# A recurrence with routed experts: when the chosen rows are numbered, fetched and turned

## The chip, the cores and the metric

The kernel runs on one core of a Trainium2 chip. The time is device microseconds of one execution; the profile is the hardware profiler's record of one execution. The core has five instruction queues that run beside each other, each in its own order: PE (matrix products and transposes), DVE (VectorE), ACT (ScalarE), POOL (GpSimd) and SP (SyncE, which here only issues DMAs). Queues wait for each other by semaphores.

## The reference, cut to what matters

Two blocks follow each other. The first is a linear-attention recurrence over 768 tokens, for 4 batches and 8 heads of width 48, with a state per head:

```
for t in range(S):
    cur   = einsum('bhd,bhe->bhde', u * k[t], v[t])
    y[t]  = einsum('bhd,bhde->bhe', r[t], state + cur)
    state = w * state + einsum('bhd,bhe->bhde', k[t], v[t])
```

The heads of y are laid side by side to x (4 batches, 768 tokens, 384 columns). The second block sends only some tokens of each batch through an MLP:

```
scores = einsum('bsd,d->bs', x, w_gate)
out = x.copy()
for b in range(B):
    top_idx = argpartition(-scores[b], capacity)[:capacity]      # capacity = 128
    xe = x[b, top_idx]
    ye = maximum(xe @ w1, 0) @ w2                                # w1: 384 x 1024
    out[b, top_idx] = xe + sigmoid(scores[b, top_idx])[:, None] * ye
```

## The kernel before, in words

**Blocks and steps.** Each batch has NC = 6 blocks of 128 tokens, so there are NU = 24 blocks. The main loop (L626) has 25 steps. Step i finishes the y of block i-1, computes scores and states of block i, turns k and r of block i+1, and works on the gate scores of blocks i-1 and i-2. Loads are issued by SP at the head of a step: k and r of block i+4 (`load_kr`, L85, L86), v of block i+3 (`load_v`, L97 or L101), in steps 4 to 12 also parts of w1 and w2 (`weights`, L208, L210), and the store of an earlier y (`store_y`, L345).

**One step, engine by engine.** PE: products from the state (L297 with z), score products k by r (`score_product`, L268), when experts are under way also state products (L278), products with the values (L297 with vin), otherwise the state products here (L292), the turn of k (L249, bank pt), the turn of r (L249, bank ea or st), pieces of the experts (`hidden`, L482; `expert`, L492), the turn of a score column (`score_row`, L379). ACT: half of the mask's diagonal (`diagonal`, L235), decays of the state (L328), copies of y (`leave_y`, L340, L341), the copy of turned k (L259). DVE: the masked copy of the scores (`masked`, L312), which writes into the mask tile `at` that ACT and POOL have filled; new states z and g (L317, L322); scaling of turned r (L254); the bonus sum `du` of the next block (L228), from which the next mask is made; the gate score (L354); comparisons of scores (L368, L385). POOL: the other half of the mask's diagonal (`diagonals`, L243, from block 4 on); then the products `kw`, `rk` and `rku` of block i+2 (L218, L222, L224).

**Choosing rows.** A token's rank in its batch is the number of scores that are at least its own. `against_earlier` and `against_own` write comparisons as 0 and 1, `count` (L395) sums them on PE, `rank` (L402, L403) adds parts of the sum on DVE, `one_hot` (L411) marks which token has which rank, `picked` (L418) turns the marks into token numbers by six small products, `index` (L424) adds their two parts to an integer, and `fetch` (L431, L432) reads the 128 rows back from `out` by an indirect DMA that POOL issues. `chosen` turns these rows on PE (L449) and copies them on ACT to `xt` (L451), and `enqueue` puts the pieces of the MLP into a queue, from which later steps take equal shares (`pieces`). `gate_sum` and `gate` (L464, L468) compute the sigmoid; `leave` (L505) and `send` (L523) add and write the rows back.

**What sets the order.** Every engine's order is the order in which the program issues instructions. Work of the second block is put into a step by hand: `at(step, place, function, ...)` files it, and `run(i, place)` issues what is filed for step i at that place. Batch b's last block is e = 6b + 5; its ranks are made in step e+3 (8, 14, 20), its rows fetched in step e+4 (9, 15, 21), its experts begun in step e+5 (10, 16, 22). The last batch is handled by code of its own behind the loop. The places of a step, in order, are "rows" (behind the masks and decays), "gate", then the masked copy and the states, "start", the turn of k, "between", the turn of r, "turned", "pick", the bonus sum, the gate score, "middle" and the rest. Whether experts are under way (`late`) is decided at the head of the step, from the queue.

PSUM banks are named; `free_bank` (L362) gives `picked`, `chosen` and `score_row` the bank ea while eb holds expert sums, and eb otherwise. A product into a bank waits until the bank's last reader is done.

Of the kernel before, what the change touches and what calls it, by code (L numbers as in the profile page):

```python
# [17 lines left out]
def kernel(  # L18
# [56 lines left out]
    def half(j):  # L75
        return slice(j * C, (j + 1) * C)

    def load_kr(n):
        b, c = divmod(n, NC)
        rows = slice(c * T, (c + 1) * T)  # L80
        if n == 0:
            KIN[n] = kws[NKW - 1][:, :, :D]
        else:
            KIN[n] = work.tile([128, H, D], F32, name="kin", bufs=NIN)
        nc.sync.dma_start(out=KIN[n], in_=k[b, :, rows, :].rearrange("h t d -> t h d"))  # L85
        nc.sync.dma_start(out=rpads[n % NIN][:, :, :D], in_=r[b, :, rows, :].rearrange("h t d -> t h d"))  # L86
# [6 lines left out]
    def load_v(n):  # L93
        b, c = divmod(n, NC)
        if n >= WHOLE:
            rows = slice(c * T, (c + 1) * T)
            nc.sync.dma_start(out=vins[n % NV][:, :, 0, :], in_=v[b, :, rows, :].rearrange("h t d -> t h d"))  # L97
            return
        for j in range(2):
            rows = slice(c * T + j * C, c * T + (j + 1) * C)  # L100
            nc.sync.dma_start(out=vins[n % NV][half(j), :, j, :], in_=v[b, :, rows, :].rearrange("h t d -> t h d"))  # L101
# [33 lines left out]
    for c in range(2):  # L135
        rows = slice(c * C, (c + 1) * C)
# [66 lines left out]
    def weights(n):  # L203
        for _ in range(n):
            j = parts.pop(0)
            if isinstance(j, tuple):
                f = slice(j[0] * F // 4, (j[0] + 1) * F // 4)
                nc.sync.dma_start(out=w1[:, j[1], f], in_=moe_w1[j[1] * 128 : (j[1] + 1) * 128, f])  # L208
            else:
                nc.sync.dma_start(out=w2[:, j, :], in_=moe_w2[j * 128 : (j + 1) * 128, :])  # L210
# [26 lines left out]
    def diagonals(n):  # L237
        if n not in AT:
            AT[n] = work.tile([128, H, C], F32, name="at", bufs=4)
        h = H // 2  # L240
        du = DU[n].rearrange("t i p -> t (i p)")
        eng = nc.gpsimd if n > 3 else nc.vector
        eng.tensor_mul(AT[n][:, h:, :], dia[:, None, :].to_broadcast([128, H - h, C]),  # L243
                       du[:, h:, None].to_broadcast([128, H - h, C]))
# [18 lines left out]
    def head(i):  # L263
        return slice(i * PAD, i * PAD + D)

    def score_product(n, hp, i, c):
        s = half(c)
        nc.tensor.matmul(out=RP[n][s, i, hp * C : (hp + 1) * C], lhsT=KH[n][head(i), hp, s],  # L268
                         rhs=RH[n][head(i), hp, s], start=True, stop=True, skip_group_check=True)
# [5 lines left out]
    def state_product(n, hp, i, c):  # L275
        if c and n % NC == NC - 1:
            return
        nc.tensor.matmul(out=RP[n][half(i), c, NP * C + hp * D : NP * C + (hp + 1) * D],  # L278
                         lhsT=kws[n % NKW][half(c), 2 * hp + i, :], rhs=vins[n % NV][half(c), 2 * hp + i, slot(n, c), :],
                         start=True, stop=True, skip_group_check=True)  # L280
# [20 lines left out]
    def from_state(n, hp, i, q):  # L301
        c = q ^ i
        z = Z1[n] if c else Z0.get(n)
        if z is not None:
            y_product(n, c, hp, i, RH[n][head(i), hp, half(c)], z[head(i), hp, :])
# [26 lines left out]
    def side(n, i):  # L332
        return YP[n][i][:, : NP * D].rearrange("t (p d) -> t p d", p=NP)
# [220 lines left out]
    def at(m, place, f, *a):  # L554
        fill.setdefault((m, place), []).append((f, a))

    def run(m, place):
        for f, a in fill.get((m, place), []):
            f(*a)
# [4 lines left out]
    for b in range(B - 1):  # L564
        e = b * NC + NC - 1
        if b:
            at(e + 3, "pick", count, b, range(NC), "st")
            at(e + 3, "middle", rank, b, ())
        else:
            at(e + 3, "turned", rank, b, range(NC), "eb")  # L570
        for z in range(NST):
            at(e + 3, "middle" if b else "turned", one_hot, b, z)
            at(e + 4, "rows", picked, b, z)
            at(e + 4, "start", index, b, z)
            at(e + 4, "start", fetch, b, z)
            at(e + 5, "between" if b else "rows", chosen, b, z)
            at(e + 5, "between" if b else "rows", enqueue, b, z)
            at(e + 5, "middle", gate_sum, b, z)
            at(e + 6, "gate", gate, b, z)

# [41 lines left out]
    def next_store(i, ahead):  # L622
        if i > 1 and ahead == ((i - 2) % NC >= NC - 2):
            store_y(i - 2)

    for i in range(NU + 1):  # L626
        next_store(i, True)
        if i + 4 < NU:
            load_kr(i + 4)
        if i + 3 < NU:  # L630
            load_v(i + 3)
        weights(WEIGHTS.get(i, 0))
        next_store(i, False)
        late = bool(queue)
        if not i:
            first()
            continue
        if i:
            if i < NU:
                t = psum.tile([128, 2, 512], F32, name="y")  # L640
                YP[i - 1] = [t[:, 0, :], t[:, 1, :]]
            else:
                YP[i - 1] = [psum.tile([128, 512], F32, name=name) for name in ("pt", "st")]
            for hp in range(NP):
                for j in range(2):
                    for q in (1, 0):
                        from_state(i - 1, hp, j, q)
            for j in range(1 if i < NU else 2):
                nc.scalar.copy(tiny[:, 1 : 1 + NP], side(i - 1, j)[C : C + 1, :, 0])
        if i < NU:  # L650
            if i not in RP:
                RP[i] = psum.tile([128, 2, 512], F32, name="rp")
            for hp in range(NP):
                for j in range(2):
                    for c in range(2):
                        score_product(i, hp, j, c)
            if late:
                for hp in range(NP):
                    for c in range(2):
                        for j in range(2):  # L660
                            state_product(i, hp, j, c)
        else:
            against_earlier(i - 2)
            score_row(i - 2, "y")
            against_own(i - 2)
            pieces(1)
        if i:
            for hp in range(NP):
                for c in range(2):
                    for j in range(2):  # L670
                        from_values(i - 1, hp, j, c)
        if i and i < NU:
            diagonal(i)
            if i > 3:
                diagonals(i)
            decays(i - 1)
            run(i, "rows")
            leave_y(i - 1)
            run(i, "gate")
        if i < NU:  # L680
            masked(i)
        if i < NU and not late:
            ST[i] = psum.tile([128, 512], F32, name="st")
            state_products(i)
        if i < NU:
            states(i)
        run(i, "start")
        if i + 1 < NU:
            if i:
                turned_k(i + 1, turn(kws[(i + 1) % NKW], "pt"))  # L690
            run(i, "between")
            turned(i + 1, turn(rpads[(i + 1) % NIN], "st" if late else "ea"))
        run(i, "turned")
        old = len(ready)
        leaving()
        m = share(i)
        if i < NU and m and (i, "pick") in fill:
            pieces(min(m, 2))
            m -= min(m, 2)
        run(i, "pick")  # L700
        if i + 1 < NU:
            bonus_sum(i + 1)
            if i < 3:
                diagonals(i + 1)
        if i and i < NU:
            gate_score(i - 1)
        run(i, "middle")
        if i < NU:
            pieces(m)
        if 2 <= i < NU:  # L710
            against_earlier(i - 2)
            score_row(i - 2, "st" if i == NC + 2 else None)
            against_own(i - 2)
        run(i, "last")
        if i + 1 < NU and not queue:
            unread(psum.tile([128, 512], F32, name="ea" if i == NC + 2 else "st"))
        run(i, "chosen")
        if i + 2 < NU:
            scaled(i + 2)
            bonus(i + 2)  # L720
        if i == 2:
            clear_v(5)
        if i == 4:
            numbers()
        send(old)
        run(i, "fetch")

    b, n = B - 1, NU - 1
# [66 lines left out]
```

## Time and profile before

| what | value |
|---|---|
| three runs | 165.79, 167.84, 171.86 us; median 167.84 us |
| the profiled execution | 168.37 us, its span 166.5 us |
| mean granted PE clock in it | 0.979 |
| busy: PE, DVE, ACT, POOL | 147.5, 117.4, 97.6, 103.5 us |
| moved by DMA | 24.13 MB, mean 145 GB/s |

How the lines are read: in a timeline or group, `L354 DVE SCALAR_TENSOR_TENSOR scr<-x,wg` is line 354 on DVE, writing tile `scr` from `x` and `wg`; ahead of it stand its start in the span and its length. `[0.91 <-POOL at L243]` says that the engine stood idle 0.91 us before it and that POOL's instruction of L243, writing `at`, ended this. PEld is the loading of weights for PE, POOLq and SPq are the queues that issue DMAs. A product in 32 bit counts as two PE instructions.

### The profile page before, as it was taken

The page shows a single profiled execution, that of the slowest core. Times are in us where ns is not written, and L with a number is a line of the kernel's source. Part 1 is how long each engine was busy: PE and PEld are TensorE (multiplying, and loading weights), DVE is VectorE, ACT ScalarE, POOL GpSimd, SP SyncE. Part 2 cuts the span into 40 slices and gives each one's busy share as a digit, 9 for nine tenths or more (in the row PEclk, how much of TensorE's full clock was granted, in tenths as well). Part 3 has the DMA queues.
Part 4 walks back from the last instruction along what each step waited for, and adds up shares of the span by engine and source line. Part 5 has one row for each costly group of instructions (what it writes and reads, how often), then busy time and mean ns, then how long its engine had stood idle before and what let it go on. Part 6 is the DMA issues. An engine that isn't in the chain of part 4 may idle for free.

```text
span 166.5 us, 8139 instructions
## 1 busy us (share of the span) xinstructions
PE 147.5 (89%) x3423; PEld 123.4 (74%) x3423; DVE 117.4 (70%) x315; ACT 97.6 (59%) x346; POOL 103.5 (62%) x138
## 2 busy tenths in 40 slices
PE   6899797999999539999979989999989799997990
PEld 3587585788788429998857869998767698746990
DVE  5659999889998924578676879866788797733010
ACT  6635787887886713476863893877648837301200
POOL 7989992999881890956682299988632831022022
PEclk9999999999999975999999999999999999999999
DMA  3999889959888778988597889999411212111000
GB/s 64 178 185 184 141 155 190 196 136 208 184 198 169 150 199 231 224 228 220 141 254 154 188 193 178 210 210 215 108 53 45 62 47 98 51 24 72 4 23 24
DMA packets 81990, 24.13 MB, mean 145 GB/s; under 512 B 75919, under 2 KB 81585, under 8 KB 81953
## 3 DMA queue, kind: packets, MB, share of 16 engines
q1 hardware_dynamic: 81404, 22.03, 63.0%
q0 software_dynamic: 544, 1.57, 3.3%
q8 instruction: 27, 0.44, 1.2%
q14 instruction: 11, 0.08, 0.2%
q10 hardware_dynamic: 4, 0.00, 0.0%
HBM read 18.09 MB, written 5.51 MB: 142 GB/s over the span
## 4 chain that ended last, share of the span: by engine, by line
PE 66%; ACT 9%; DVE 6%; issue 6%; DMA 6%; POOL 4%; POOLq 1%; ACTq 0%; DVEq 0%
PE y L297 12%; PE eb L482 7%; PE pt L249 7%; PE ea L482 6%; PE rp L268 6%; DMA xr<-out_dram,idx 6%; PE ea L492 5%; PE st L292 5%; PE eb L492 4%; PE ea L249 3%; ACT z L328 3%; PE rp L278 3%; PE st L249 3%; PE st L272 3%; ACT at L235 3%
## 5 line engine op out<-in xcount | busy, mean ns | idle before, releaser
L243 POOL TENSOR_TENSOR at<-dia,du 128x256 f32<-128x256 f32 x20 | 14.8, 739 | 25.1 <-DVE du L228 19.7
L312 DVE COPY_PREDICATED at<-mask,rp 128x512 f32<-128x512 uint32 x24 | 17.8, 740 | 13.9 <-ACT at L235 6.0
L235 ACT ACTIVATE at<-dia,du 128x64 f32<-128x64 f32 x96 | 25.5, 336 | 1.7 <-DVE du L228 1.7
L224 POOL TENSOR_TENSOR rku<-rk,ub 128x384 f32<-128x384 f32 x24 | 24.9, 1039 | 1.9
L218 POOL TENSOR_TENSOR kw<-kin,wk 128x384 f32<-128x384 f32 x23 | 24.2, 1051 | 0.6 <-ACT wk L590 0.4
L222 POOL TENSOR_TENSOR rk<-rpad,kin 128x384 f32<-128x384 f32 x23 | 23.4, 1018 | 0.0
L354 DVE SCALAR_TENSOR_TENSOR scr<-x,wg 128x384 f32<-128x384 f32 x24 | 21.5, 895 | 1.0 <-ACT x L341 0.6
L328 ACT ACTIVATE z<-g,wc 128x48 f32<-128x48 f32 x80 | 19.9, 320 | 0.5 <-DVE wc L616 0.5
L249 PE MATMUL pt<-ident,kw 128*128 128x128 f32 x96 | 17.2, 304 | 1.8 <-issue 1.4
L268 PE MATMUL rp<-rh,kh 48*64 48x64 f32 x768 | 17.4, 225 | 0.1
L297 PEld LDWEIGHTS y<-z,rh 48*64 48x64 f32 x672 | 12.8, 134 | 6.3 <-ACT kh L259 2.4
L432 POOL DMA_INDIRECT xr<-out_dram,idx x4 | 4.1, 1029 | 19.3 <-DVE part L500 9.7
L297 PE MATMUL y<-vin,at 64*64 64x48 f32 x736 | 16.1, 220 | 0.0
L259 ACT COPY kh<-pt 128x512 f32<-128x512 f32 x23 | 13.6, 590 | 3.7 <-PE pt L249 3.7
L297 PE MATMUL y<-z,rh 48*64 48x48 f32 x672 | 15.6, 223 | 0.0
L268 PEld LDWEIGHTS rp<-rh,kh 48*64 48x64 f32 x768 | 14.7, 138 | 0.7 <-DVE rh L254 0.4
L340 ACT COPY x<-y 64x192 f32<-64x192 f32 x46 | 14.4, 313 | 1.2 <-PE y L297 0.4
L249 PEld LDWEIGHTS pt<-ident,kw 128*128 128x128 f32 x96 | 11.0, 150 | 5.0 <-issue 2.0
L297 PEld LDWEIGHTS y<-vin,at 64*64 64x64 f32 x736 | 13.7, 135 | 0.0
L482 PE MATMUL eb<-xt,w 128*128 128x128 f32 x96 | 13.1, 293 | 0.5 <-ACT xt L451 0.5
L482 PEld LDWEIGHTS eb<-xt,w 128*128 128x128 f32 x96 | 12.4, 209 | 0.8 <-ACT xt L451 0.8
L228 DVE TENSOR_REDUCE du<-rku 128x8 f32<-128x384 f32 x24 | 13.0, 543 | 0.0
(171 smaller groups left out, 295.3 us busy)
## 6 DMA issues: line engine op xcount, KB each, us to landing
rpad<-in_r_dram SPq DMA_DIRECT2D x24, 192.0 KB, 4.9
out_dram<-x SPq DMA_DIRECT2D x24, 192.0 KB, 3.7
kin<-in_k_dram SPq DMA_DIRECT2D x23, 192.0 KB, 4.6
vin<-in_v_dram SPq DMA_DIRECT2D x13, 192.0 KB, 5.1
vin<-in_v_dram SPq DMA_DIRECT2D x22, 96.0 KB, 4.2
w<-in_moe_w_dram SPq DMA_DIRECT2D x12, 128.0 KB, 3.3
w<-in_moe_w_dram SPq DMA_DIRECT2D x8, 192.0 KB, 4.2
kw<-in_k_dram SPq DMA_DIRECT2D x1, 192.0 KB, 3.1
```

What stands on the lines that cost most here:

```text
L218: (nc.gpsimd if n else nc.vector).tensor_mul(kws[n % NKW][:, :, :D], KIN[n], wk)
L222: nc.gpsimd.tensor_mul(rk, rpads[n % NIN][:, :, :D], KIN[n])
L224: nc.gpsimd.tensor_mul(RKU[n], rk, ub)
L235: nc.scalar.activation(AT[n][:, j, :], dia, AF.Copy, scale=du[:, j : j + 1])
L249: nc.tensor.transpose(t[:, hp, :], x[:, 2 * hp : 2 * hp + 2, :], ident)
L268: nc.tensor.matmul(out=RP[n][s, i, hp * C : (hp + 1) * C], lhsT=KH[n][head(i), hp, s], rhs=RH[n][head(i), hp, s], start=True, stop=True, s ...
L297: nc.tensor.matmul(out=YP[n][i][half(c ^ i), hp * D : (hp + 1) * D], lhsT=lhsT, rhs=rhs, start=(c, i) not in started, stop=True, skip_grou ...
L312: nc.vector.copy_predicated(at, causal, RP[n][:, :, : NP * C].rearrange("s i (p t) -> s i p t", p=NP))
L328: nc.scalar.activation(Z0[n + 1][:, hp, :], G[n][:, hp, :], AF.Copy, scale=wc[:, hp : hp + 1])
L354: nc.vector.scalar_tensor_tensor(scr, X[n], 1.0, wg, op0=OP.mult, op1=OP.mult, accum_out=sc[b][:, c : c + 1])
L482: nc.tensor.matmul(out=PE[b, z][:, f % 4, :], lhsT=w1[:, d, f * 128 : (f + 1) * 128], rhs=XT[b, z][d], start=(d == 0), stop=(d == KD - 1))
L492: nc.tensor.matmul(out=pe[:, : cols.stop - cols.start], lhsT=HT[b, z][:, f, :], rhs=w2[:, f, cols], start=(f == 0), stop=(f == FB - 1))
```

## The change

Seven filings change their place, and two places are new: "scored" directly behind the score products, and "bonus" directly behind the bonus sum, ahead of the gate score.

```diff
@@ filing, for each of the first three batches
         if b:
             at(e + 3, "pick", count, b, range(NC), "st")
-            at(e + 3, "middle", rank, b, ())
+            at(e + 3, "bonus", rank, b, ())
         else:
             at(e + 3, "turned", rank, b, range(NC), "eb")
         for z in range(NST):
-            at(e + 3, "middle" if b else "turned", one_hot, b, z)
-            at(e + 4, "rows", picked, b, z)
-            at(e + 4, "start", index, b, z)
-            at(e + 4, "start", fetch, b, z)
-            at(e + 5, "between" if b else "rows", chosen, b, z)
-            at(e + 5, "between" if b else "rows", enqueue, b, z)
+            at(e + 3, "bonus" if b else "turned", one_hot, b, z)
+            at(e + 4, "scored", picked, b, z)
+            at(e + 4, "scored", index, b, z)
+            at(e + 4, "scored", fetch, b, z)
+            at(e + 5, "between", chosen, b, z)
+            at(e + 5, "between", enqueue, b, z)
@@ behind the score products of step i
+            run(i, "scored")
             if late:
@@ behind the bonus sum of step i
             if i < 3:
                 diagonals(i + 1)
+        run(i, "bonus")
         if i and i < NU:
             gate_score(i - 1)
         run(i, "middle")
```

In issue order this means: in steps 14 and 20, DVE gets the ranks and the one-hot ahead of the gate score and the comparisons (step 8 keeps its order). In steps 9, 15 and 21, PE gets the picking product ahead of the value products (and, where experts are under way, ahead of the state products), DVE gets the index ahead of the masked copy, and POOL gets the fetch ahead of its half of the mask. In step 10, PE gets the turn of the chosen rows, and ACT their copy, behind the turn of k instead of ahead of the state products; in steps 16 and 22 they stood there before. No instruction is added or taken away.

## The prediction

> Steps are turns i of the main loop; a step starts with its first product from the state (L297). In the profile step 9 starts at 50.42 us, 10 at 55.12, 11 at 68.38, 15 at 90.61, 16 at 95.19, 17 at 102.34, 21 at 123.90, 22 at 128.63, 23 at 135.72.
>
> **What bounds the kernel now.** First the page: PE is busy 89% of the span, so what matters is where it is not. Second, the busy times in stretches cut at the starts of steps (sum, then PE, PEld, DVE, ACT, POOL busy; granted clock; DMA share; GB/s):
>
> ```profile
> 50.40:55.10 4.70, 4.45 (x130) 3.69 (x129) 4.07 (x13) 3.65 (x14) 1.26 (x3) 1.00 0.77 156
> 55.10:68.40 13.30, 9.05 (x147) 8.21 (x146) 8.03 (x18) 4.14 (x15) 9.13 (x10) 0.74 0.87 206
> 68.40:73.70 5.30, 5.30 (x144) 5.06 (x147) 3.52 (x10) 4.34 (x16) 3.15 (x5) 1.00 1.01 249
> ...
> 95.20:102.30 7.10, 6.19 (x159) 5.43 (x158) 6.15 (x13) 4.20 (x15) 6.92 (x8) 1.00 0.83 174
> 102.30:107.60 5.30, 5.30 (x145) 5.02 (x143) 5.17 (x17) 4.34 (x16) 4.92 (x7) 1.00 1.13 198
> ...
> 128.60:135.70 7.10, 5.98 (x159) 5.26 (x158) 6.16 (x14) 4.13 (x15) 4.00 (x5) 1.00 0.27 88
> ```
>
> Ordinary steps with expert work take 5.3 us with PE full. Step 10 takes 13.3, and at a granted clock of 0.74; steps 16 and 22, which also begin a batch's expert work, take 7.1. Third, the chain of waits in step 10 (start, length, what):
>
> ```profile
> 52.44 1.98 issue
> 54.42 0.02 POOLq L218
> 54.44 0.23 issue
> 54.67 6.26 DMA xr<-out_dram,idx
> 60.93 0.14 issue
> 61.06 0.87 PE eb L449 x3
> ```
>
> POOL stands 1.98 us waiting for the index, the rows take 6.26 us to land, and PE, which meets their turn (L449) ahead of its own state products, idles 4.25 us and then runs at half clock until about 66. Fourth, the chain in step 16:
>
> ```profile
> 96.33 0.81 ACT at L235 x3
> 97.14 0.90 ACT z L328 x4
> ...
> 99.04 0.49 ACT kh L259
> 99.53 0.46 ACT xt L451
> 99.98 0.04 issue
> 100.03 2.28 PE ea L482 x18
> ```
>
> Here it is ScalarE's queue that ends last: masks (L235), decays, two copies of y, k's copy, then xt, which the expert's first products need. From the mask's start (96.08) to those products is 3.95 us, and 2.31 more to the next step (102.34). Step 22 reads the same (129.52, 133.41, 135.72). ScalarE's mask waits for DVE's bonus sum (L228). Fifth, the timeline around the fetch:
>
> ```profile
> 54.67 1.17 POOL L432 DMA_INDIRECT xr<-out_dram,idx  x1 [2.23 <-DVE idx L424]
> 55.35 2.91 DVE L354 SCALAR_TENSOR_TENSOR scr<-x,wg 128x384 f32<-128x384 f32 x1
> 59.08 0.61 POOL L243 TENSOR_TENSOR at<-dia,du 128x256 f32<-128x256 f32 x1
> 59.71 0.73 DVE L312 COPY_PREDICATED at<-mask,rp 128x512 f32<-128x512 uint32 x1 [0.91 <-POOL at L243]
> ...
> 91.84 0.35 DVE L385 SCALAR_TENSOR_TENSOR gt<-ea,sc,tri 128x128 bf16<-128x128 f32 x1
> 92.62 0.30 PE L418 MATMUL ea<-tok,oh 128*128 128x2 bf16 x6
> 92.65 0.74 DVE L312 COPY_PREDICATED at<-mask,rp 128x512 f32<-128x512 uint32 x1 [0.45 <-ACT at L235]
> ```
>
> The masked copy needs POOL's half of the mask (L243) and starts 0.02 us after it. The change puts the fetch, with its wait, ahead of that half on POOL's queue.
>
> **Batch 0, steps 9 and 10.** No instruction is added or removed. The picking product needs the one-hot (ends 51.00) and follows the score products (end 51.58): at about 51.5, 0.30 long. The index follows DVE's L385 readout, at 52.2 instead of 54.23. An index's start leads the fetch's by 0.44 (54.23 to 54.67): fetch at 52.6. Behind it on POOL, 1.21 later (54.67 to 55.88), stands the mask half: 53.8 to 54.4; so the masked copy is at 54.45 instead of 52.71. Behind that copy DVE holds z (+0.85), g (+0.39), r's scaling (+0.28), the bonus sum (+0.60, 0.54 long), all by the rows of steps 8 and 9: the sum ends at 57.1 instead of 55.43. ScalarE's mask follows 0.10 later, at 57.2; plus 3.95, the expert products start at 61.2. PE: scaled r is ready at 56.7, score products to 57.3, values 57.9, state products 58.7, k's turn 59.3, the rows' turn 59.8, r's turn 60.3; it waits for xt, not for the rows, if these land by 59.3. With before's 6.26 us they land at 58.9, with the median of 3.7 at 56.3. So step 11 starts at 61.2 + 2.31 = 63.5 instead of 68.38: **-4.9 us**: the 4.25 of idling, the half clock behind it, less the later mask. The gaps left on PE are under 1 us; I count the clock as full, as it was over the 1.4 us gap at 86.4.
>
> A rule can be set beside the landing: the Trainium skill, DMA: Bandwidth & Descriptors, "Queues, rings and completion order", has each engine take turns between the queues at packet granularity, so a backlog on SP's queue should hardly hold the fetch. The rows say otherwise: 6.26 us here among loads, 2.95 in the tail without them. The sum is the same by either (55.6 or 58.9 against 59.3); I take the row.
>
> **Batch 1, steps 14 to 16.** The ranks move ahead of the gate score (L354), but the count on PE sets their time (L402 waited 0.17 for it), so the one-hot still ends at 91.91; L354 and L385 now stand behind it, L385 at 92.33 to 92.68 instead of 91.84. The picking product uses the bank that L385 reads (ea), so it cannot start at the score products' end (91.6), but at 92.75: PE stands about 1.1 us, with the state products and values behind it. They are not on the chain. Index 93.15 (before 94.16), fetch 93.6, mask half 94.6 to 95.2, masked copy 95.23 instead of 92.65, bonus sum to 97.9 instead of 95.37, ScalarE's mask at 98.0 instead of 96.08 (there it waited for PE). The rest of step 16 is ScalarE's 3.95 and 2.31: **+1.9**. The rows land around 98 and are not the limit. Steps 17 to 19 are full of PE work, so this is not won back.
>
> **Batch 2, steps 20 to 22.** The same: L385 to 125.97, index 126.4, masked copy 128.5, bonus sum to 131.16, ScalarE's mask 131.26 instead of 129.52: **+1.75**.
>
> **The gate score** ran 2.70 to 2.91 us after each fetch instead of 0.55, until 0.4 us after POOL's L222 had ended. The Trainium skill, GPSIMD Engine Reference, "1. Specifications", says that POOL shares SBUF interfaces with VectorE and contends with instructions of two SBUF inputs, as L354 is; it gives no time, and speaks against the change as well, since POOL's products now still run when L354 starts: bonus sum and POOL both count from the mask half, L354 comes 2.6 us after it, L224 ends after 3.0. Which row? At 25.11 an L354 that began under L224 took 1.35, to 0.4 us past its end: then it takes 0.8 here and hides beside ScalarE's chain, cost 0. By the fetch rows it is held to the end of the next L222, 2.6 us more (a rival below). I take the first, whose neighbour it is. That today's stretch goes gains nothing: ScalarE ends later.
>
> **Turning batch 0's rows later, enqueueing later:** in the above. The bank (eb) was last read by L385 (58.4), before 59.3.
>
> **Loads.** SP issues without a pause from 50 to 85 us, about one step behind PE, so its times will not move up with PE. Against a need 4.4 us earlier I compared issue plus landing (page, section 6): the third quarter of w1 (issued by 62.2, landing 3.3 to 5.7 later) is there by 65.5 to 67.9, needed 67.3; v of block 15 (81.8 + 5.1) 86.9, needed 88.6; block 11's store, which batch 1's fetch must follow, (84.0 + 3.7) 87.7 against 89.2. Between 0 (all in time) and 4.9 (all given back) I take **+0.5**, near the low end since most margins are positive.
>
> **Sum** against the profiled execution, 168.37 us (span 166.5 and 1.9 around it): -4.9 + 1.9 + 1.75 + 0.5 = -0.75, so **167.6 us**. It lies 0.3% above the median of the runs shown (167.84), which then stands for no change.
>
> **Rivals.** (1) Loads set the pace, the slower side: the stretch 55 to 79 moved loads at a share of 0.80 to 1.01 of the DMA engines; squeezed by 4.9 us it would need more than they have. If steps 11 to 15 then wait for v, k or weights by 4.9 in sum, only the prices stay: 168.37 + 3.65 = 172.0. It decides from the point where SP falls two steps behind PE; for it speak the margins of 2 us and less, against it that loads are asked for three and four steps ahead. (2) L354 held to the next L222: the rows' turn waits for L385: 1.4 more in step 10, 1.0 in 16, none in 22, where POOL has no further products: 170.0. For it: the three fetch rows; against: all other meetings ended at the next boundary. (3) The prices of batches 1 and 2 aren't paid, as ScalarE's late mask finds slack: 168.37 - 4.9 + 0.5 = 164.0. Against it: the chain in steps 16 and 22 is without a gap.
>
> **Chances.** Forecast 0.45, loads 0.20, L354 0.20, no price 0.15. Each scatters by some 1.5 us. Range 164.0 to 172.0 takes in all four; the forecast's own is 166.0 to 169.2. About 2% (3.4 us) is what a measurement of this kernel can tell: slower than 171.2 is three quarters of the loads case, a third of L354 and a sliver of the forecast, 0.24; faster than 164.5 is 0.6 of the no-price case and a sliver, 0.10; within, 0.66.
>
> **What would show it.** Right: step 10 near 8 us at full clock, no wait of PE for xr; steps 16 and 22 near 9; POOL's mask half directly behind each fetch and the masked copy waiting 1.5 to 2 us for it; L418 waiting for L385 in steps 15 and 21. Wrong: PE waits for vin, kw or w in steps 11 to 15; L354 still at 2 us or more; a half clock in step 9 or 10.

## The result, and the profile after

The changed kernel takes 173.91 us in the median (173.04 to 174.69, 4 executions); the kernel before, on the same chip, 167.39. The ratio is **1.042**, 95% interval 1.032 to 1.052: it is slower. The forecast of 167.6 and its whole range (164.0 to 172.0) lie below. (Ratios here and below are formed from the undisturbed executions of either kernel, medians from all.) The profiled execution took 173.04 us, its span 171.3.

First the stretches between the starts of steps, as before (9, 10, 14, 15, 16, 21, 22; sum, then PE, PEld, DVE, ACT, POOL busy; granted clock; DMA share; GB/s):

```profile
50.14:56.28 6.14, 4.55 (x130) 3.75 (x130) 3.95 (x13) 3.72 (x14) 3.86 (x5) 1.00 0.77 160
56.28:63.37 7.09, 6.17 (x144) 5.59 (x143) 6.14 (x18) 3.87 (x14) 6.57 (x7) 1.00 0.88 206
79.79:88.34 8.55, 6.44 (x163) 4.70 (x162) 3.43 (x11) 3.58 (x13) 3.03 (x5) 0.82 0.96 229
88.34:96.68 8.34, 8.09 (x148) 6.76 (x148) 5.02 (x16) 3.85 (x14) 4.83 (x6) 0.57 0.93 190
96.68:103.77 7.09, 5.75 (x159) 5.28 (x159) 5.38 (x16) 4.14 (x15) 5.08 (x6) 1.00 0.83 186
124.68:133.27 8.59, 7.11 (x148) 5.19 (x147) 5.65 (x18) 3.75 (x14) 5.40 (x6) 0.80 0.17 52
133.27:140.37 7.10, 5.75 (x160) 5.29 (x159) 5.12 (x14) 4.14 (x15) 1.55 (x3) 1.00 0.09 31
```

Steps 9 and 10 together went from 17.96 to 13.23 us: batch 0's part is there. Steps 16 and 22, where the forecast put the price (near 9), kept their 7.1. The loss is in steps 15 and 21, 4.6 and 4.7 before, and in step 14, 6.55 before. With it comes half clock, from 85.3 to 95.6 us and from 129.7 to 133.1. The forecast named each time of steps 9 and 10; step 9 starts 0.28 us earlier than before, and counted from there the times agree to about 0.3 us:

```profile
52.31 1.17 POOL L432 DMA_INDIRECT xr<-out_dram,idx  x1 [3.02 <-DVE idx L424]
53.52 0.62 POOL L243 TENSOR_TENSOR at<-dia,du 128x256 f32<-128x256 f32 x1
54.17 0.74 DVE L312 COPY_PREDICATED at<-mask,rp 128x512 f32<-128x512 uint32 x1 [2.16 <-POOL at L243]
...
56.05 0.54 DVE L228 TENSOR_REDUCE du<-rku 128x8 f32<-128x384 f32 x1
...
56.51 1.03 DVE L354 SCALAR_TENSOR_TENSOR scr<-x,wg 128x384 f32<-128x384 f32 x1
...
61.05 2.16 PE L482 MATMUL eb<-xt,w 128*128 128x128 f32 x17 [0.92 <-ACT xt L451]
```

PE no longer waits for the rows, the expert products start at 61.05 (forecast 61.2), step 11 at 63.37 (63.5), and L354 takes 1.03 us where it took 2.91. Now step 21, where the time was lost, first before:

```profile
125.33 0.80 PE L297 MATMUL y<-vin,at 64*64 64x48 f32 x32
...
126.06 0.30 PE L418 MATMUL eb<-tok,oh 128*128 128x2 bf16 x6
...
127.14 1.46 PE L492 MATMUL ea<-w,ht 128*128 128x384 f32 x4
```

and after:

```profile
125.18 0.66 PE L268 MATMUL rp<-rh,kh 48*64 48x64 f32 x32
...
125.91 0.55 DVE L354 SCALAR_TENSOR_TENSOR scr<-x,wg 128x384 f32<-128x384 f32 x1
...
126.39 0.35 DVE L385 SCALAR_TENSOR_TENSOR gt<-eb,sc,tri 128x128 bf16<-128x128 f32 x1
...
126.80 0.29 PE L418 MATMUL eb<-tok,oh 128*128 128x2 bf16 x6 [0.96 <-DVE gt L385]
...
127.52 0.94 PE L297 MATMUL y<-vin,at 64*64 64x48 f32 x25
...
128.88 0.35 PE L297 MATMUL y<-vin,at 64*64 64x48 f32 x7 [0.42 <-issue]
...
130.46 2.77 PE L492 MATMUL ea<-w,ht 128*128 128x384 f32 x4
```

Read downwards: PE is through with the score products by 125.84, and the picking product stands for 0.96 us until the comparison L385 has been read out of the bank (eb) that it wants to write. The value products, 0.80 us before, then take 1.71 with holes in them (pauses that no semaphore explains), and the two expert products (four instructions), 1.46 before, take 2.77. The reason for the last is in the clock column of the stretches around them, cut here at 3.41 us; in every trace here whose clock falls inside the loop, it stays down for whole multiples of that length:

```profile
122.82:126.23 3.41, 3.02 (x90) 2.23 (x89) 2.87 (x7) 1.97 (x8) 0.20 (x2) 1.00 0.19 62
126.23:129.64 3.41, 2.32 (x74) 2.01 (x74) 1.09 (x7) 1.66 (x8) 2.06 (x3) 1.00 0.12 25
129.64:133.06 3.42, 3.42 (x11) 2.06 (x9) 3.08 (x9) 1.08 (x3) 3.34 (x4) 0.51 0.27 97
```

In the middle stretch PE is busy 2.32 of 3.41 us (2.39 if it is cut at 129.71, where the clock falls), and the whole next one runs at half clock.

Step 15 of this profile reads differently: it begins at half clock, which lasts from step 14 to 95.6, and its picking product at 90.31 shows no wait. So the wait is read here in step 21, and in step 15 from the other kernels below that have it.

### The profile page after: what moved, and what is told of

Read it like the earlier page. It is cut to its first block, busy times and chain, and to the rows that moved or that the text cites. A ratio compares the mean times of both kernels' runs of the same rounds, so it can differ in the third digit from the quotient of the medians.

```text
span 171.3 us, 8140 instructions
## 1 busy us (share of the span) xinstructions
PE 151.0 (88%) x3423; PEld 124.7 (73%) x3423; DVE 111.2 (65%) x315; ACT 97.7 (57%) x346; POOL 103.7 (61%) x138
## 4 chain that ended last, share of the span: by engine, by line
PE 58%; ACT 11%; issue 9%; POOL 8%; DVE 8%; DMA 4%; POOLq 1%; SPq 0%; ACTq 0%; DVEq 0%
PE y L297 11%; PE eb L482 6%; PE ea L482 6%; PE ea L492 5%; PE pt L249 5%; PE rp L268 4%; PE eb L492 4%; ACT z L328 3%; ACT at L235 3%; PE st L249 3%; PE rp L278 3%; PE ea L249 2%; PE st L292 2%; DMA w<-in_moe_w_dram 2%; PE st L272 2%
## 5 line engine op out<-in xcount | busy, mean ns | idle before, releaser
L312 DVE COPY_PREDICATED at<-mask,rp 128x512 f32<-128x512 uint32 x24 | 17.8, 741 | 21.5 <-ACT at L235 12.5
L243 POOL TENSOR_TENSOR at<-dia,du 128x256 f32<-128x256 f32 x20 | 15.3, 765 | 19.9 <-DVE du L228 16.5
L224 POOL TENSOR_TENSOR rku<-rk,ub 128x384 f32<-128x384 f32 x24 | 24.1, 1006 | 1.9
L297 PE MATMUL y<-vin,at 64*64 64x48 f32 x736 | 17.6, 224 | 1.6 <-issue 1.5
L297 PEld LDWEIGHTS y<-vin,at 64*64 64x64 f32 x736 | 14.7, 138 | 2.3 <-issue 2.2
L354 DVE SCALAR_TENSOR_TENSOR scr<-x,wg 128x384 f32<-128x384 f32 x24 | 15.6, 652 | 1.0 <-ACT x L341 0.6
L482 PE MATMUL eb<-xt,w 128*128 128x128 f32 x96 | 12.2, 278 | 2.3 <-ACT xt L451 2.3
L482 PE MATMUL ea<-xt,w 128*128 128x128 f32 x96 | 12.5, 279 | 1.5 <-ACT xt L451 1.3
L649 ACT COPY tiny<-y 1x4 f32<-1x4 f32 x23 | 3.6, 156 | 17.9 <-PE y L297 17.9
```

What stands on the lines that cost most here:

```text
L224: nc.gpsimd.tensor_mul(RKU[n], rk, ub)
L297: nc.tensor.matmul(out=YP[n][i][half(c ^ i), hp * D : (hp + 1) * D], lhsT=lhsT, rhs=rhs, start=(c, i) not in started, stop=True, skip_grou ...
L312: nc.vector.copy_predicated(at, causal, RP[n][:, :, : NP * C].rearrange("s i (p t) -> s i p t", p=NP))
L354: nc.vector.scalar_tensor_tensor(scr, X[n], 1.0, wg, op0=OP.mult, op1=OP.mult, accum_out=sc[b][:, c : c + 1])
L482: nc.tensor.matmul(out=PE[b, z][:, f % 4, :], lhsT=w1[:, d, f * 128 : (f + 1) * 128], rhs=XT[b, z][d], start=(d == 0), stop=(d == KD - 1))
```

## The experiments

Two theories stood at the start. A: the moves of batches 1 and 2 themselves cost the time, by PE's wait for the comparison, by what follows it on PE and its clock, or by the late mask; the later runs part these. B: batch 0's part squeezes the loads, and they take the time. Edits are shown against the changed kernel. "Bank wait" is the wait of PE's L418 for L385.

**1. Batch 0's part alone.**

```diff
-            at(e + 3, "bonus", rank, b, ())
+            at(e + 3, "middle", rank, b, ())
-            at(e + 3, "bonus" if b else "turned", one_hot, b, z)
-            at(e + 4, "scored", picked, b, z)
-            at(e + 4, "scored", index, b, z)
-            at(e + 4, "scored", fetch, b, z)
+            at(e + 3, "middle" if b else "turned", one_hot, b, z)
+            at(e + 4, "rows" if b else "scored", picked, b, z)
+            at(e + 4, "start" if b else "scored", index, b, z)
+            at(e + 4, "start" if b else "scored", fetch, b, z)
```

> Only batch 0 is changed (steps 9 and 10); ranks, picks, fetches of batches 1 and 2 stay where they were before. The two traces differ by step: 9 +1.4, 10 -6.2, 12 and 13 +0.7, 14 +2.0, 15 +3.8, 21 +3.9 us. Theory A, the price lies in the batches' own steps 15 and 21: only -4.8 in steps 9 and 10 stays, ratio 0.97. Theory B, the loads: squeezing steps 10 to 14 makes PE's stall in step 14 longer and drops its clock in steps 14 and 15: +0.7, +2.0 and some 1.9 of step 15 come along, ratio 1.00, step 14 at 8.5 us.

Measured: 167.28 us (164.84 to 170.4, 4 executions) against 167.68 before. Two executions took 165.41 and 164.84, two 169.16 and 170.4, too few for a ratio. In the profile (span 163.6) steps 9 and 10 take 6.22 and 7.09, as in the changed kernel, steps 15 and 21 5.54 and 4.78; step 15 has a hole of 0.70 us in its state products without any wait before it. So the slowness is not in batch 0's part. But that part does not bring 4.9 us either: 0.4 in the median, some 2 in the two shorter executions.

**2. Batches 1 and 2 alone.**

```diff
-            at(e + 4, "scored", picked, b, z)
-            at(e + 4, "scored", index, b, z)
-            at(e + 4, "scored", fetch, b, z)
-            at(e + 5, "between", chosen, b, z)
-            at(e + 5, "between", enqueue, b, z)
+            at(e + 4, "scored" if b else "rows", picked, b, z)
+            at(e + 4, "scored" if b else "start", index, b, z)
+            at(e + 4, "scored" if b else "start", fetch, b, z)
+            at(e + 5, "between" if b else "rows", chosen, b, z)
+            at(e + 5, "between" if b else "rows", enqueue, b, z)
```

> Only batches 1 and 2 are changed, batch 0 as before: step 10 keeps its 13 us. Theory A: steps 15 and 21 each 3.8 longer, +7.7 us, ratio 1.046. Theory B: step 14 as before (6.5), so step 15 at full clock, 6.5 instead of 8.3; step 21 still +3.9; together +5.8, ratio 1.035.

Measured: 173.79 us (171.41 to 174.29, 6 executions), ratio 1.038 (1.034 to 1.042). Nearly the whole slowdown is here. In its profile steps 15 and 21 take 6.92 and 8.53, both with a bank wait of 0.96 us, steps 16 and 22 7.10 and 7.09, and step 14 6.82: the 8.55 of step 14 in the profile of the changed kernel is not needed for a loss. The profiled execution (171.41 us, mean clock 0.976) is the shortest of the six; the others have 0.941 to 0.960, so they ran longer at half clock, where isn't on record.

**3. Another bank for the picking product.** Bank st is free at that point; nothing waits there for the comparison.

```diff
-            at(e + 4, "scored", picked, b, z)
+            at(e + 4, "scored", picked, b, z, "st" if b else None)
```

> The changed kernel with the picking product of batches 1 and 2 in bank st, which the score comparison doesn't read. If PE's wait for that comparison (0.96 us in step 21) is what drops the clock there: step 21 falls from 8.6 to about 6.2 and holds full clock; step 15, whose clock fell already in step 14, by 0.5 to 1 only; 3 us less than the changed kernel, ratio to before 1.02. If the late masked copy behind the fetch drops it: nothing moves, ratio 1.04.

Measured: 168.11 us (165.35 to 171.43, 12 executions), ratio 1.000 (0.994 to 1.006): the slowdown is gone, more of it than was expected (1.02), by a change of nothing but the bank. Steps 15 and 21 take 5.21 and 5.20 at full clock, the bank wait has become one of 0.21 us for the one-hot. Steps 16 and 22 now show a price, 7.60 in both. Its profiled execution, 169.17 us, also holds a stretch that nobody expected, in step 9:

```profile
50.26 0.15 DVE L424 TENSOR_REDUCE idx<-eb 128x1 int32<-128x2 f32 x1
...
54.65 1.18 POOL L432 DMA_INDIRECT xr<-out_dram,idx  x1 [2.64 <-DMA kin<-in_k_dram]
55.86 0.62 POOL L243 TENSOR_TENSOR at<-dia,du 128x256 f32<-128x256 f32 x1
56.52 0.73 DVE L312 COPY_PREDICATED at<-mask,rp 128x512 f32<-128x512 uint32 x1 [6.12 <-POOL at L243]
```

The index is there at 50.41, but the fetch starts 4.24 us later, the mask half stands behind it, and DVE waits 6.12 us for it; step 9 takes 11.20 us. The records name a load as what ended part of that wait; the store of batch 0's last block, which a fetch must follow, may be the rest.

**4. The fetch behind POOL's mask half.**

```diff
-            at(e + 4, "scored", fetch, b, z)
+            at(e + 4, "rows", fetch, b, z)
```

> The changed kernel with the fetch issued behind POOL's half of the mask; picking product and index stay early. If POOL's late mask half is the price: the masked copy comes about 2 us sooner in steps 9, 15 and 21, step 9 back at 4.8, steps 15 and 21 by about 2 shorter each, 5 us less than the changed kernel, ratio 1.01. If PE's wait for the comparison and the clock are the price: steps 15 and 21 stay above 8, ratio 1.03 to 1.04.

Measured: 172.82 us (171.4 to 173.91, 4 executions), ratio 1.034 (1.027 to 1.040). The late mask, on which the whole price of the forecast rested, is taken away, and steps 15 and 21 stay at 8.54 and 8.56, with a bank wait of 0.96 us and half clock in both. What it does bring is in step 9: 5.42 instead of 6.14.

**5. The ranks back behind the gate score.** The picking product keeps the bank of the comparison, but the comparison is earlier.

```diff
-            at(e + 3, "bonus", rank, b, ())
+            at(e + 3, "middle", rank, b, ())
-            at(e + 3, "bonus" if b else "turned", one_hot, b, z)
+            at(e + 3, "middle" if b else "turned", one_hot, b, z)
```

> The changed kernel with ranks and one-hot of batches 1 and 2 back behind the gate score. The one-hot ends at the same time (the count on PE sets it), the comparison that holds the picking product's bank ends about 0.5 us sooner. If PE's wait for that bank is the whole price: steps 15 and 21 lose 0.5 us each, ratio to before 1.035. If a shorter wait also keeps the clock full: they fall from 8.5 to about 6, ratio 1.01.

Measured: 165.9 us (163.54 to 167.43, 11 executions) against 165.66, ratio 1.004 (0.997 to 1.011). PE still waits for the comparison, 0.27 us in step 15 and 0.57 in step 21, there 0.39 less than in the changed kernel, and nothing follows from it:

```profile
123.53 0.29 PE L418 MATMUL eb<-tok,oh 128*128 128x2 bf16 x6 [0.57 <-DVE gt L385]
123.75 0.68 PE L278 MATMUL rp<-vin,kw 64*64 64x48 f32 x32
124.25 0.67 PE L297 MATMUL y<-vin,at 64*64 64x48 f32 x32
```

The values take 0.67 us without a hole, the clock is full, step 21 takes 5.48 instead of 8.60: 3.1 us for 0.39 of waiting. Step 14 takes 9.03 us here, with half clock, in a kernel as fast as before. This execution, 167.4 us, is among the longest of the eleven, so the stretch in step 14 bears on single executions; that it makes the difference between the kernels isn't shown.

**6 and 7. PE kept busy.** The idle time is filled by eight, in a later run by three, useless products ahead of the picking product, whose results nobody reads. Nothing can start earlier by them.

```diff
+    def busy(n):
+        p = psum.tile([128, 4, 128], F32, name="pt")
+        for j in range(n):
+            nc.tensor.matmul(out=p[:, j % 4, :], lhsT=ident, rhs=ident, start=True, stop=True, skip_group_check=True)
...
+            if b:
+                at(e + 4, "scored", busy, 3)
             at(e + 4, "scored", picked, b, z)
```

> The changed kernel with 8 products of no use ahead of the picking product in steps 15 and 21, into bank pt, which is free there: PE is busy for about 1 us of the time in which it now waits for the comparison. If the dropped clock is a good part of the price of step 21 (3.4 us of half clock, some 1.7 us): step 21 at full clock and 1.5 to 2 us shorter, ratio 1.02. If the wait itself and what queues behind it is the price: 0 to 0.5 us longer, ratio 1.04.

> The changed kernel with 3 useless products (into the bank of the turn, which nobody reads before it is written again) on PE ahead of the picking products of batches 1 and 2: they should last some 0.75 us, about what PE stands idle there (8 of them took 2.05). Nothing starts earlier by them. Theory A: PE has nearly no hole, the clock stays, values take 0.67 us, steps 15 and 21 at 5.3 to 6.0 us, the whole near 167.5. Rival (the price is the later start of values and states, not the hole): steps 15 and 21 stay at 7.9 to 8.6, the whole at 173 to 174.

Measured with eight: 168.51 us (167.36 to 171.96, 4 executions), ratio 1.019 (1.010 to 1.027) to 165.66. With three: 167.72 (165.4 to 172.49, 4 executions) against 166.36, too few for an interval. The timeline of step 21 with three (L564 are the useless ones):

```profile
122.01 0.94 PE L564 MATMUL pt<-ident 128*128 128x128 f32 x6
...
122.63 0.35 DVE L385 SCALAR_TENSOR_TENSOR gt<-eb,sc,tri 128x128 bf16<-128x128 f32 x1
...
123.04 0.29 PE L418 MATMUL eb<-tok,oh 128*128 128x2 bf16 x6
...
123.76 0.67 PE L297 MATMUL y<-vin,at 64*64 64x48 f32 x32
...
125.29 1.46 PE L492 MATMUL ea<-w,ht 128*128 128x384 f32 x4
```

And its steps 21 and 22:

```profile
120.92:126.78 5.86, 5.77 (x154) 4.67 (x153) 3.43 (x13) 3.76 (x14) 2.96 (x4) 1.00 0.17 53
126.78:134.18 7.40, 5.96 (x159) 5.40 (x158) 7.23 (x21) 4.21 (x15) 3.99 (x6) 1.00 0.13 45
```

The comparison is just as late, and the picking product starts 2.12 us after the step's start, as in the changed kernel (126.80 - 124.68). Yet the values take 0.67 us, the experts 1.46, the clock is full, and step 21 is 2.7 us shorter. Step 15 takes 5.88; it is best set beside that of experiment 2, which has the wait at full clock (6.92), and is 1.0 shorter. With eight the picking product of step 21 is even later (2.98 us after the step's start), and the step, 6.73, is still shorter than in the changed kernel. So in step 21 the larger part of the loss is not that PE's work starts later, but what PE's idling does to the time of the work behind it; in step 15, where the clock held, it is the smaller part.

**8. Ranks early, all else as before the change.**

```diff
-            at(e + 4, "scored", picked, b, z)
-            at(e + 4, "scored", index, b, z)
-            at(e + 4, "scored", fetch, b, z)
-            at(e + 5, "between", chosen, b, z)
-            at(e + 5, "between", enqueue, b, z)
+            at(e + 4, "rows", picked, b, z)
+            at(e + 4, "start", index, b, z)
+            at(e + 4, "start", fetch, b, z)
+            at(e + 5, "between" if b else "rows", chosen, b, z)
+            at(e + 5, "between" if b else "rows", enqueue, b, z)
```

> Only the ranks and one-hots of batches 1 and 2 move ahead of the gate score; the picking products, index and fetch stay where they were before the change. Theory A (the price is PE standing for the comparison L385 in the middle of its work, and the clock that falls behind it): L385 is as late as in the changed kernel, but the picking product meets it only behind the value products, where PE has 0.3 us or less to wait; steps 15 and 21 stay at 4.6 to 4.8 us, the whole as before, 167.5. Rival (the later comparison and gate score cost in themselves, wherever the picking product stands): steps 15 and 21 at 6 or more, 170 or more.

Measured: 165.61 us (164.85 to 167.78, 4 executions) against 166.36, ratio 1.010 (0.994 to 1.026, wide); steps 15 and 21 take 5.06 and 4.67. In this profile the late comparison costs at most half a microsecond by itself: in step 21 it is read out at 122.49, the picking product starts at 122.54. It takes both moves, the comparison later and the picking product earlier, to make the wait.

**9. Batch 0's part alone, with its fetch behind the mask half.** As in experiment 1, and:

```diff
-            at(e + 4, "start" if b else "scored", fetch, b, z)
+            at(e + 4, "start" if b else "rows", fetch, b, z)
```

> Only batch 0 changed (as in the run with the first batch alone), with its fetch behind POOL's half of the mask. If the early fetch's wait is what that run's slower executions pay (a late store holds the fetch, and the mask behind it): step 9 at 5.4 instead of 6.2 us, executions closer together, ratio 0.97 to 0.98. If the loads are what they pay: no change, ratio near 1.0.

Measured: 164.62 us (162.63 to 166.73, 22 executions) against 165.66, ratio 1.002 (0.996 to 1.009). In the profile (span 161.7) steps 9 and 10 take 4.64 and 7.09, 6.2 us less than before. Steps 11 to 13 take 18.3 us, 2.7 more than before; PE waits there for weights by 1.8 us and POOL for k by 6.7. Step 14 takes 8.46, 1.9 more, with a stall of PE that no wait explains and half clock behind it. So 4.6 of the 6.2 us are handed back, 2.7 of them in the steps with the waits for loads, and no difference is left that could be told.

**10. Own bank, and the fetch behind the mask half.**

```diff
-            at(e + 4, "scored", picked, b, z)
+            at(e + 4, "scored", picked, b, z, "st" if b else None)
-            at(e + 4, "scored", fetch, b, z)
+            at(e + 4, "rows", fetch, b, z)
```

> The changed kernel with both mends: picking product of batches 1 and 2 in bank st, every fetch behind POOL's mask half. If the two prices are the bank and the queue on POOL: steps 15 and 21 at 4.7 to 5.0, 9 at 5.4, 16 and 22 at 7.1, and the 6 us of step 10 stay gained: ratio 0.97. If something else takes them back: ratio near 1.0 as in the run with the bank alone.

> The kernel of the run with its own bank and the fetch behind the mask half once more, in five rounds, since it was measured 1.1% faster than before from few executions while its sister with the ranks behind the gate score came out at no difference. If that gain was real: ratio 0.985 to 0.995, median near 163.5. If it was the luck of few executions and the loads take back what batch 0 brings (as in steps 11 to 13 of the sister, 19.0 us against 16.4): ratio 0.997 to 1.007. In the profile either way: steps 9 and 10 at 4.65 and 7.1, steps 15 and 21 at 5.1, steps 16 and 22 at 7.1.

> The best so far (picking products of batches 1 and 2 in a bank of their own, fetch behind POOL's half of the mask) with the ranks behind the gate score again, as before the change. Theory A: with the bank free, the place of the ranks doesn't matter: steps 15, 21 at 5.1, 16, 22 at 7.1, the whole within 1 us of 163.2. Rival (the earlier ranks are part of what made that kernel faster): 1 us or more above it.

Measured: 163.16 us (162.0 to 164.5, 4 executions), ratio 0.989 (0.983 to 0.995); again, with more: 164.55 (162.19 to 167.38, 22 executions) against 165.62, ratio **0.996** (0.992 to 1.000). With the ranks put back: 165.3 (162.95 to 167.48, 11 executions), ratio 1.004 (0.997 to 1.011). In all three profiles steps 9, 10, 15, 16, 21, 22 take 4.6, 7.1, 5.1, 7.1, 5.1, 7.1; what differs are steps 11 to 13, with 16.4, 17.8 and 19.0 us in sum, and PE's and POOL's waits for weights, k and r in them. So this version beats the changed kernel clearly, and the one before by half a per cent if at all. The third run missed its expectation, being 2.1 us above the first; but the repeat is 1.4 above it too, so the first, with its four executions, was lucky. The ranks don't show in it, for steps 15 and 21 read the same.

## Why the prediction was wrong

**The step that failed** is in "Batch 1, steps 14 to 16": "PE stands about 1.1 us, with the state products and values behind it. They are not on the chain." The wait was seen, with its place, its cause and nearly its length (0.96 us), and then costed at nothing, since ScalarE's chain, late by the mask, was to end last anyway. The runs show in its place: taking this wait away by another bank, with all else kept, takes the slowdown away (experiment 3); filling it with three useless products takes 2.7 us from step 21 (experiment 7). Its price is not its length. Step 21 of the changed kernel is 3.87 us longer than before: 1.1 is what the step with three useless products loses too (5.86 against 4.73); of the other 2.7, 1.0 are the holes in the values, 1.3 the expert products and 0.4 the turn of r at half clock. Where the clock holds, in step 15 of experiment 2, the step is still 2.3 us longer than before, and 1.0 of it are the holes (the values take 1.73 us).

**"I count the clock as full"**, said of step 10 and silently carried to 15 and 21, is the other half of the same failure. The argument was one gap of 1.4 us at 86.4 that left the clock alone. In step 10 it held. It did not follow that 0.96 would be harmless elsewhere: in the three profiles with that wait (changed kernel, experiments 2 and 4) the clock fell behind it in every step 21, and in one of the two steps 15 that show it.

**The late mask** came, but the forecast sized its price too high and put it in the wrong place. Its chain can be followed where PE doesn't idle. With three useless products the bonus sum of step 21 starts 6.43 us after the step's start (127.35 - 120.92), and ScalarE's mask of step 22 directly behind it:

```profile
127.98 1.07 ACT L235 ACTIVATE at<-dia,du 128x64 f32<-128x64 f32 x4 [0.24 <-DVE du L228]
```

The forecast had the sum at 6.72 (131.16 less its own 0.54, from 123.90). Steps 21 and 22 are there 1.44 us longer than before (13.26 against 11.82), forecast 1.75; steps 15 and 16 1.55, forecast 1.9. But this is not the mask's price alone: PE, busy without a pause, makes step 21 1.1 us longer by itself, and the mask adds 0.3 in step 22. Experiment 3 and the first version of experiment 10 differ only in whether the fetch stands ahead of the mask half or behind it: steps 21 and 22 take 12.80 against 12.19 us, steps 15 and 16 12.81 against 12.20. So without the wait the late mask costs 0.6 us per batch. In the changed kernel steps 16 and 22 show none of it, because the longer step ahead gives the mask its time: two delays side by side, of which the longer counts. So the rival without a price was right that the mask would find slack there, and wrong on the total, for the slack was made by the other delay.

**Batch 0's part was right in the profile** (step 11 at 63.37) and the L354 rival is out: 1.03 us, near the forecast's 0.8. But the 4.9 were taken off one execution, whose step 10 had 6.8 us of half clock (60.5 to 67.3, and not only until about 66, as the prediction reads it). Steps 9 and 10 took 17.96 us there; in two other profiles with the same order, of experiments 2 and 8, 14.7 and 16.2. Then the loads: steps 11 to 13, 15.7 us before, take 16.4 to 19.0 in the four profiles of experiments 9 and 10, with waits for weights and k in three of them. So the loads rival had a true part: more than the forecast's +0.5 is given back there in some executions. It isn't what made the kernel slower, since experiment 3 kept batch 0's part and its loads and ended level.

**Not foreseen, and open:** step 14 of the changed kernel's profile has a stall of PE of 2.11 us in the turn of k that no semaphore explains ("issue"), and three intervals of half clock behind it. The same stall, 0.55 to 2.48 us, is in every profile here, in before as well (1.39), and it is followed by half clock in three (the changed kernel and experiments 5 and 9). Step 14 is 2.0 us longer by it than before in this profile, and the half clock reaches through most of step 15. The slowdown does not need it (experiment 2's profile), and a kernel can have it and be as fast as before (experiment 5). What it comes from was not settled, nor what makes the holes in the values: they stand behind every wait of 0.96 us, but the hole of 0.70 us in experiment 1 has no wait ahead of it.

## What to carry to other kernels

Before an instruction is moved forward on PE, look up who last reads the bank that it writes, and where that reader stands after all other moves: here neither of two moves alone cost anything that could be told (experiments 5 and 8), and the pair made a wait of 0.96 us, with which step 21 was 3.9 longer. A wait of the matrix engine is not free because another chain is longer; ask what its clock does in the next interval, and test it cheaply, with another bank or with useless products that fill the gap. And a gain read off one execution's worst stretch is worth what that stretch is worth in the others.

## What the runs showed of the hardware

The clock's steps sit on a grid of 3.41 us: inside the loop each half clock lasted one, two or three such lengths (3.4, 6.8, 10.2), and its starts in one trace are whole multiples apart (85.33 and 129.71 in the changed kernel, 13.0 lengths). The Trainium skill, TensorE: Matmul & The Clock Gate, "What's actually happening", has the clock fall after at least one idle window of about 3.4 us. The length agrees with the traces, the idleness doesn't: the window ahead of the fall in step 21 had PE busy for about 2.4 of 3.41 us. How busy is enough can't be read from PE's busy share alone. A second window with the same wait and a fall behind it, from experiment 4 (step 21):

```profile
124.62:128.03 3.41, 2.41 (x75) 2.11 (x75) 1.31 (x8) 1.70 (x8) 2.11 (x3) 1.00 0.13 26
128.03:131.45 3.42, 3.42 (x10) 1.96 (x8) 2.54 (x9) 0.99 (x3) 2.62 (x3) 0.50 0.26 96
```

In step 15 of experiment 2, with the same wait, the window on that trace's own grid (89.92 to 93.33; its falls are at 59.19 and 127.46) has PE busy for 2.64 us, and the clock stays. That would fit a limit between the two. But a window of step 22 in the changed kernel has less than either, and keeps its clock:

```profile
136.47:139.88 3.41, 2.06 (x19) 1.83 (x17) 3.34 (x10) 1.51 (x5) 1.06 (x3) 1.00 0.17 60
```

Its work is the experts' large products, that of the others mostly the small ones of 48 to 64 rows. That alone is not the difference, for the window of the kernel before with the gap of 1.4 us in step 14 has almost nothing but small ones, and keeps its clock in the next as well:

```profile
84.33:87.74 3.41, 2.08 (x127) 1.89 (x118) 2.32 (x7) 2.83 (x12) 3.19 (x4) 1.00 1.08 260
87.74:91.15 3.41, 3.36 (x69) 2.62 (x72) 2.16 (x7) 1.02 (x3) 0.80 (x2) 1.00 0.85 166
```

What decides it stays open.
